# Local and global attention on one Trainium2 core: windows of 96 keys with the 32 global keys beside them as 128 rows

## The chip, the core and the metric

The kernel runs on one core of one Trainium2 chip. Its time is the device time of one execution in microseconds (us). The core has five engines that run side by side: TensorE (PE, with its weight loads PEld), VectorE (DVE), ScalarE (ACT), GpSimd (POOL) and SyncE (SP), which here issues the transfers between the memory of the chip and the on-chip memory. Matmuls write into the accumulator memory PSUM, of 8 banks; DVE and ACT read it from there.

## What is computed

Eight batches of eight heads, 512 local and 32 global tokens, 64 columns a head. A local query sees the 32 global keys and the local keys up to 32 positions away; a global query sees all 544 keys. What comes out is the input of a feed-forward layer with a gate, which is most of the work and isn't touched by the change.

```python
def _attn_ref(q_l, k_l, v_l, q_g, k_g, v_g):
    window = 32
    scale = 1.0 / np.sqrt(D)
    k_all = np.concatenate([k_g, k_l], axis=2)
    v_all = np.concatenate([v_g, v_l], axis=2)
    s_g = scale * np.matmul(q_g, k_all.transpose(0, 1, 3, 2))
    out_g = np.matmul(sm(s_g), v_all)
    s_ll = scale * np.matmul(q_l, k_l.transpose(0, 1, 3, 2))
    mask = np.abs(pos[:, None] - pos[None, :]) <= window
    s_ll = np.where(mask, s_ll, -1000000000.0)
    s_lg = scale * np.matmul(q_l, k_g.transpose(0, 1, 3, 2))
    a_l = sm(np.concatenate([s_lg, s_ll], axis=-1))
    out_l = np.matmul(a_l, np.concatenate([v_g, v_l], axis=2))
    return np.concatenate([out_g, out_l], axis=2)

def _moe_ref(x, mu_k, mu_r, w_k, w_v, w_r):
    xk = mu_k * x + (1.0 - mu_k) * x_prev
    xr = mu_r * x + (1.0 - mu_r) * x_prev
    k = np.maximum(xk @ w_k, 0.0)
    v = k * k @ w_v
    return 1.0 / (1.0 + np.exp(-(xr @ w_r))) * v
```

## The kernel before

**Units and pairs.** A unit is two heads of one batch: 32 units, 4 a batch. Two units are handled together as a pair (`attention`, L761), 16 pairs in all. The first batch is done by halves of the queries at the start (L851 on), while the weights are still coming in. From the second batch on, the attention of one batch runs beside the feed-forward part of the batch ahead: `together` (L804) hands out the steps of the two in turn, and a scheduler then orders each engine's instructions. `Run` (L354) ties the matmuls of one stage into a run that stands on TensorE without others in between; from the third batch on its first matmul waits for the readers that it is given.

**Scores** (`scores`, L308). A unit's 512 queries are 8 blocks of 64 (`BL`), each against a window of 128 local keys and the 32 global ones, 160 columns (`WG`). A matmul has 64 rows (one head's columns) by 64 queries as its weights and streams the 160 keys; two heads and two blocks use the four quarters of the array. A unit has 16 such matmuls, in four PSUM banks. DVE adds the mask, takes the row's lowest value and evacuates (L333); ACT takes the exponentials and their sum (L339); POOL multiplies by the inverse sum (L349), for the window into `Pt` and, apart from it, for the 32 global columns into `Pgl`.

**Transposes.** For each unit TensorE transposes 8 tiles of `Pt` (L394) and 2 of `Pgl` (L403), and copies bring them into `PT` and `PTg`. `scores_global` (L411) makes the scores of the global queries of both units, in 576 columns; `transposes_global` (L438) transposes them as 5 tiles into `PG`.

**Weighted sums** (`weighted`, L450). With a window's values as weights (128 keys by 64 columns of one head) a matmul streams 64 columns of `PT`; 32 of them a pair. 20 more, with the same kind of weights, stream 32 columns of `PG` for the global queries, and 8, with the global values as weights, stream 128 columns of `PTg` for the global keys' part. ACT and DVE copy the results into `xT` and `xg_all`, the feed-forward layer's input.

**Transfers.** SP issues, in order, `raw_qk` and `raw_v` for each unit, pieces `a` of the value weights from `scratch`, and the output. Only `kernel` on the host lays out keys and values: windows overlap, so values are stored more than once.

**Names in the profile.** L508 to L510 and L670 are the feed-forward matmuls. L361, L365 and L367 are the three calls in `Run.matmul`, so that all matmuls of scores and weighted sums stand under these lines: `ps<-raw_qk` are scores, `PT,raw_v`, `PG,raw_v` and `PTg,raw_v` the three kinds of weighted sums.

Of the kernel before, what the change touches and what calls it, by code (L numbers as in the profile page):

```python
# [9 lines left out]
F32 = mybir.dt.float32  # L10
# [9 lines left out]
P = 128  # L20
D = 64
SG = 32
SL = 512
BL = 64
NB = SL // BL
W = 128
WG = W + SG

SPANS = ((0, W), (32, 224), (160, 352), (288, 480), (SL - W, SL))
START = tuple(224 * (i // 2) + (128 if i % 2 else 0) for i in range(NB))
SK = START[-1] + WG

FIRST = tuple(min(max(BL * i - SG, 0), SL - W) for i in range(NB))

PAIRS = tuple(tuple((e + 4 * p, e + 4 * p + 2) for p in range(2)) for e in range(2))
# [3 lines left out]


VG0 = 2 * NB * D
VX0 = VG0 + 2 * D
NV = VX0 + 2 * D
# [10 lines left out]
def local_global_attention_then_rwkv_ffn(  # L56
# [61 lines left out]
    masks = const.tile([P, 2, 2, WG], BF16, name="masks")  # L118
    nc.gpsimd.memset(masks, 0.0)
    for e in range(2):  # L120
        for p in range(2):
            for a, i in enumerate(PAIRS[e][p]):

                m = masks[a * BL:(a + 1) * BL, e, p, SG * e:SG * e + W]
                ahead = FIRST[i] - BL * i + SG
                nc.gpsimd.affine_select(
                    out=m, in_=m, pattern=[[1, W]], base=ahead, channel_multiplier=-1,
                    compare_op=ALU.is_ge, fill=NEG,
                )
                nc.gpsimd.affine_select(  # L130
                    out=m, in_=m, pattern=[[-1, W]], base=2 * SG - ahead, channel_multiplier=1,
                    compare_op=ALU.is_ge, fill=NEG,
                )

    low = const.tile([P, 3 * W], BF16, name="low")
    nc.gpsimd.memset(low[:, 0:SG], NEG)
    nc.gpsimd.memset(low[:, SG:], 0.0)
# [15 lines left out]
    for side, n in (("left", 16), ("right", 104)):  # L153
        shift = ctx.enter_context(tc.tile_pool(name=f"shift_{side}", bufs=1, side=side))
        shift.tile([P, n], F32, name=f"shift_{side}")
# [129 lines left out]
    def load_v(s, pool=rawp, tag=""):  # L285
        raw = pool.tile([P, NV], F32, tag="v" + tag, name="raw_v")
        nc.sync.dma_start(out=raw, in_=v[s.b, s.c])
        s.v = raw[:, 0:VG0].rearrange("p (h i d) -> p h i d", h=2, d=D)
        s.vg = raw[:, VG0:VX0]
        s.vx = raw[:, VX0:NV].rearrange("p (h d) -> p h d", h=2)  # L290
# [9 lines left out]
    EACH = [(e, t, h, 4 * e + 2 * t + h) for t in range(2) for e in range(2) for h in range(2)]  # L300

    class Scores:
        def __init__(self, slots):
            self.slots = slots
            for t, (s, p) in enumerate(slots):
                s.at[p] = self, t
# [753 lines left out]
```

## Time and profile before

| | us |
|---|---|
| median of 3 runs | 691.82 |
| the runs | 690.74, 691.82, 691.88 |
| span of the profiled execution, first to last instruction | 689.8 |
| TensorE clock granted in it, mean share | 0.992 |

No time of its own is kept for the profiled execution; its span is 2.0 us below the median of the runs. The page's second part shows that TensorE and its weight loads are dense from the second slice of 17 us to the last, and that the transfers come in bursts:

```profile
PE   6979999999998999999999999999999999999997
PEld 3769789989897999999999989999999999999997
DVE  5795977457557566545675657645575656377531
DMA  8734353154737740544818092735727090535666
```

Each digit is the busy share of a fortieth of the span in tenths. In what follows, a row of a group reads: line, engine, operation, output and inputs, shape and count, then busy time in us, mean ns of one, and idle time of the engine ahead of them with what ended it.

### The profile page before, as it was taken

The numbers are of one execution on the slowest core, as the hardware profiler recorded it, in microseconds if no ns is written. First come the engines' busy times: TensorE is split into PE (matmuls) and PEld (weight loads), VectorE is DVE, ScalarE is ACT, GpSimd is POOL, SyncE is SP. The second block draws the span as 40 slices with busy tenths as digits, with TensorE's granted clock in tenths as the row PEclk, the third lists the DMA queues.
The fourth block names the chain that finished last, engine by engine and source line by source line (L and its number), as shares of the span: only waits on it lengthen the run. The fifth ranks groups of instructions, "written<-read, shape, count | busy, mean of one in ns | idle before, by whom it ended". The sixth has DMA issues, their size and how long they took to land.

```text
span 689.8 us, 18729 instructions
## 1 busy us (share of the span) xinstructions
PE 663.3 (96%) x7530; PEld 626.6 (91%) x7530; DVE 425.9 (62%) x1221; ACT 387.5 (56%) x1058; POOL 359.4 (52%) x363
## 2 busy tenths in 40 slices
PE   6979999999998999999999999999999999999997
PEld 3769789989897999999999989999999999999997
DVE  5795977457557566545675657645575656377531
ACT  5876866366355565757457563747466644443530
POOL 5577595147777344565338244655348332642810
PEclk9989999999999999999999999999999999999999
DMA  8734353154737740544818092735727090535666
GB/s 343 299 122 169 124 196 127 48 185 141 254 131 253 248 157 29 210 159 151 310 67 302 12 358 92 263 105 204 256 97 271 2 334 34 200 119 172 207 197 208
DMA packets 43542, 123.37 MB, mean 179 GB/s; under 512 B 4032, under 2 KB 20928, under 8 KB 43456
## 3 DMA queue, kind: packets, MB, share of 16 engines
q1 hardware_dynamic: 43456, 122.18, 50.0%
q8 instruction: 59, 0.97, 0.5%
q14 instruction: 27, 0.22, 0.1%
HBM read 104.86 MB, written 17.30 MB: 177 GB/s over the span
## 4 chain that ended last, share of the span: by engine, by line
PE 67%; DVE 12%; POOL 7%; DMA 6%; issue 3%; ACT 3%; SPq 0%; POOLq 0%; ACTq 0%; DVEq 0%
PE ps_m L670 16%; PE ps_m L508 11%; PE ps_m L509 11%; PE ps_m L510 11%; PE ps_s L365 9%; DMA a<-scratch 4%; PE ps_t L394 3%; DVE xfull L539 2%; DVE Pt L333 2%; PE ps_t L361 2%; DVE diff L535 2%; PE ps_s L367 2%; DMA w<-w_k 1%; DVE B L651 1%; POOL Pt L349 1%
## 5 line engine op out<-in xcount | busy, mean ns | idle before, releaser
L508 PE MATMUL ps_m<-xkh,wk_h 128*128 128x256 f32 x544 | 154.3, 285 | 3.3 <-DVE xfull L539 3.3
L509 PE MATMUL ps_m<-xkl,wk_h 128*128 128x256 f32 x544 | 153.2, 282 | 1.0 <-POOL xkl L544 1.0
L510 PE MATMUL ps_m<-xkh,wk_l 128*128 128x256 f32 x544 | 152.5, 281 | 0.0
L670 PE MATMUL ps_m<-bh,a 128*128 128x256 f32 x736 | 137.5, 282 | 3.2 <-DMA a<-scratch 3.1
L339 ACT ACTIVATE Pt<-Pt,m 128x160 f32<-128x160 f32 x256 | 106.5, 419 | 26.7 <-DVE m L333 26.7
L670 PEld LDWEIGHTS ps_m<-bh,a 128*128 128x128 f32 x736 | 114.9, 188 | 6.1 <-DMA a<-scratch 3.7
L349 POOL TENSOR_TENSOR Pt<-Pt,ssum 128x512 f32<-128x512 f32 x64 | 67.4, 1053 | 80.7 <-DVE ssum L295 32.4
L508 PEld LDWEIGHTS ps_m<-xkh,wk_h 128*128 128x128 f32 x544 | 103.0, 190 | 4.9 <-ACT xkh L543 3.8
L509 PEld LDWEIGHTS ps_m<-xkl,wk_h 128*128 128x128 f32 x544 | 102.8, 189 | 2.5 <-POOL xkl L544 1.7
L510 PEld LDWEIGHTS ps_m<-xkh,wk_l 128*128 128x128 f32 x544 | 102.8, 189 | 0.0
L670 PE MATMUL ps_m<-bl,a 128*128 128x256 f32 x368 | 102.5, 279 | 0.0
L544 POOL TENSOR_TENSOR xkl<-xfull,xkh 128x512 fp32r<-128x512 f32 x34 | 46.8, 1375 | 85.9 <-ACT xkh L543 80.9
L582 DVE TENSOR_TENSOR B<-ps_m,relu 128x512 f32<-128x512 f32 x52 | 35.9, 690 | 72.1 <-ACT relu L580 72.0
L580 ACT ACTIVATE relu<-ps_m 128x512 f32<-128x512 f32 x52 | 31.0, 597 | 82.9 <-PE ps_m L510 80.7
L508 PE MATMUL ps_m<-xrh,wr_h 128*128 128x256 f32 x272 | 77.3, 284 | 0.0
L509 PE MATMUL ps_m<-xrl,wr_h 128*128 128x256 f32 x272 | 76.2, 280 | 0.0
L510 PE MATMUL ps_m<-xrh,wr_l 128*128 128x256 f32 x272 | 76.0, 279 | 0.0
L333 DVE CUSTOM_DVE_ANT_0 Pt<-ps_s,masks 128x160 f32<-128x160 f32 x256 | 65.9, 317 | 6.6 <-PE ps_s L365 4.9
L670 PEld LDWEIGHTS ps_m<-bl,a 128*128 128x128 f32 x368 | 69.2, 188 | 0.0
L617 POOL TENSOR_TENSOR gate<-sum,gate 128x512 f32<-128x512 f32 x18 | 26.8, 1489 | 59.7 <-DVE sum L716 39.9
L205 ACT CAST bh<-B 128x512 fp32r<-128x512 f32 x76 | 45.9, 620 | 18.0 <-PE ps_m L670 11.6
L508 PEld LDWEIGHTS ps_m<-xrh,wr_h 128*128 128x128 f32 x272 | 51.5, 189 | 1.2 <-ACT kkh L564 0.6
(146 smaller groups left out, 1594.6 us busy)
## 6 DMA issues: line engine op xcount, KB each, us to landing
a<-scratch SPq DMA_DIRECT2D x92, 512.0 KB, 5.9
raw_qk<-qk SPq DMA_DIRECT2D x32, 768.0 KB, 5.6
raw_v<-v SPq DMA_DIRECT2D x32, 640.0 KB, 6.0
out_l<-gate SPq DMA_DIRECT2D x32, 256.0 KB, 4.6
w<-w_k SPq DMA_DIRECT2D x8, 512.0 KB, 9.7
w<-w_v SPq DMA_DIRECT2D x8, 512.0 KB, 3.9
w<-w_r SPq DMA_DIRECT2D x4, 512.0 KB, 3.5
scratch<-wv_h SPq DMA_DIRECT2D x8, 256.0 KB, 2.8
```

The costliest lines, as they stand in the source:

```text
L205: nc.scalar.copy(hi, val)
L333: read = nc.vector.tensor_tensor_reduce(out=Pt[:, i], in0=place(e, t, h), in1=masks[:, e, slots[t][1]], op0=ALU.add, op1=ALU.min, scale=-s ...
L339: nc.scalar.activation(Pt[:, i], Pt[:, i], AF.Exp, bias=low_x[:, i:i + 1], scale=-1.0, accum_out=ssum[:, i:i + 1],)
L349: nc.gpsimd.tensor_mul(out, Pt[:, each, at:at + n], rinv.unsqueeze(2).to_broadcast([P, 4, n]))
L365: self.last = nc.tensor.matmul(*a, **kw)
L508: nc.tensor.matmul(out, w_h[:, i, cols], x_h(i), start=(i == 0), stop=False)
L509: nc.tensor.matmul(out, w_h[:, i, cols], x_l(i), start=False, stop=False)
L510: nc.tensor.matmul(out, w_l[:, i, cols], x_h(i), start=False, stop=(i == n - 1))
L544: nc.gpsimd.tensor_sub(lo[:, both], xf, hi[:, both].bitcast(F32))
L580: nc.scalar.activation(rk, kp, AF.Relu)
L582: nc.vector.tensor_mul(k2[f0 // HC][f0 % HC // 2], kp, rk)
L670: nc.tensor.matmul(out[:, j], w, x[:, i % 2], start=fresh and (i, j, n) == (0, 0, 0), stop=(i, n) == (HC - 1, 2), skip_group_check=True,)
```

## The change

The 512 local tokens become 16 chunks of 32 (`CK`). On the host, keys and values are laid out in one order, three local chunks, then the 32 global ones, then the next three (`ORDER`), so that any four consecutive chunks are three local chunks and the global one: 14 windows of 128 rows (`START`), one for each local chunk but the two at the ends, which share their neighbour's. A query chunk's window holds all that it sees.

```diff
-BL = 64
-W = 128
-WG = W + SG
+CK = 32
+NCK = SL // CK
+W = 4 * CK
+ORDER = [x for c in range(0, NCK, 3) for x in (*range(c, min(c + 3, NCK)), None)][:-1]
+SK = CK * len(ORDER)
+NW = NCK - 2
+START = tuple(CK * (w + w // 3) for w in range(NW))
+def window_of(i):
+    return min(max(i - 1, 0), NW - 1)
+ROWS = ((2, 3, 0, 1), (4, 5, 6, 7), (8, 9, 10, 11), (14, 15, 12, 13))
-NV = VX0 + 2 * D
+NV = 2 * NW * D
```

`raw_qk` goes from 1536 to 1248 columns and `raw_v` from 1280 to 1792, of 4 bytes on 128 rows each.

A scores matmul now has 32 queries as weights and streams 128 keys; four query chunks (`ROWS`) stand in the four column groups of the array, and a unit needs two PSUM banks where it needed four. Masks are built chunk by chunk.

```diff
-        banks = [psum("s") for _ in range(4)]
+        banks = [psum("s") for _ in range(2)]
...
-                            place(e, t, h)[a * BL:(a + 1) * BL], s.q[rows, i * BL:(i + 1) * BL],
-                            s.k[rows, START[i]:START[i] + WG], start=True, stop=True,
+                            place(t, n, h)[r_ * CK:(r_ + 1) * CK], s.q[rows, i * CK:(i + 1) * CK],
+                            s.k[rows, at:at + W], start=True, stop=True,
...
-            window = Pt[:, each, SG * e:SG * e + W]
-            for out, at in ((window, SG * e), (Pgl[:, e], 0 if e else W)):
-                n = out.shape[2]
-                nc.gpsimd.tensor_mul(out, Pt[:, each, at:at + n], rinv.unsqueeze(2).to_broadcast([P, 4, n]))
+            nc.gpsimd.tensor_mul(
+                Pt[:, each], Pt[:, each], all_inv[:, each].unsqueeze(2).to_broadcast([P, 4, W])
+            )
```

`Pgl`, `PTg` and `transposes_of_g` are gone. `PT` is one fixed tile for both units, with room between its blocks for the transposed scores of the global queries (`TAIL`), which are copied in there: six transposes, of 96 keys or 128, each key once (544 columns where 576 were). In `weighted` a window's values are loaded once and stream the columns of the chunks that use the window, and behind them, in six of the 14 windows, the 32 of the global queries (`GROUPS`; `cells` makes an access of two blocks that lie apart).

```diff
-        windows(0)
-        og = global_ones() if PG is not None else None
-        windows(1)
-        for j, s in enumerate(units):
-            for e in range(2):
-                for p in pairs:
...
-                        op[t][:, j, e], s.vg[rows], r.PTg[rows, e], start=False,
+            for w, here, t in GROUPS:
...
+                    if len(here) == 1 and t is not None:
+                        i, = here
+                        moving = cells(P_of, PLACE[i], TAIL[t] - PLACE[i], 2)
+                        out = cells(out, of.index(i) * CK, (of.index(None) - of.index(i)) * CK, 2)
...
+                    run.matmul(out, s.v[:, h, w], moving, start=first, stop=True, skip_group_check=True)
```

In `attention` the scores of both units of the next pair are one run, and the scores of its global queries stand in one run with the weighted sums of this pair:

```diff
-            if nxt:
-                R.append(scores(whole(nxt[0])))
...
             if nxt:
-                R.append(scores(whole(nxt[1])))
-                Pg = scores_global(nxt)
+                run = run_of(nxt[0])
+                R = [scores(whole(s), run) for s in nxt]
             yield
+            yield
+            run = run_of(pair[0], A.copies + C.copies + copies)
             with tc.issue_after(last.ins):
-                weighted(pair, xTs, PG,
-                         copies=A.copies + C.copies + [copy] if pair[0].b > 1 else None)
+                if nxt:
+                    Pg = scores_global(nxt, run=run)
+                weighted(pair, xTs, PG, run=run)
```

What this makes of the order of instructions is shown at three places. First TensorE at the weighted sums of a pair in the middle of the program: before, the scores of the global queries (64 by 160, 32 and 384), the three kinds of weighted sums, and a unit's first transposes.

```order
L367 MATMUL ps_s<-raw_qk 64x160
L365 MATMUL ps_s<-raw_qk 64x160
L365 MATMUL ps_s<-raw_qk 64x32 x2
L365 MATMUL ps_s<-raw_qk 64x384 x2
L367 MATMUL ps_s<-PT,raw_v 64x64
L365 MATMUL ps_s<-PT,raw_v 64x64 x15
L365 MATMUL ps_s<-PG,raw_v 64x32 x20
L365 MATMUL ps_s<-PT,raw_v 64x64 x16
L365 MATMUL ps_s<-PTg,raw_v 128x2x64 x8
L394 MATMUL ps_t<-ident,Pt 128x128 x4
```

At the same place now (L371 and L373 are the lines of `Run.matmul` after the change, L703 is a feed-forward matmul):

```order
L373 MATMUL ps_s<-raw_qk 64x480
L371 MATMUL ps_s<-raw_qk 64x480
L371 MATMUL ps_t<-raw_qk 64x64 x2
L371 MATMUL ps_s<-PT,raw_v 64x96 x2
L371 MATMUL ps_s<-PT,raw_v 64x2x32 x8
L371 MATMUL ps_s<-PT,raw_v 64x96 x2
L371 MATMUL ps_s<-PT,raw_v 64x32 x32
L371 MATMUL ps_s<-PT,raw_v 64x96 x2
L371 MATMUL ps_s<-PT,raw_v 64x2x32 x8
L371 MATMUL ps_s<-PT,raw_v 64x96 x2
L703 MATMUL ps_m<-bh,a 128x256
```

60 weighted matmuls of the pair have become 56; the products with `PG` and `PTg` have gone into those with `PT`, and feed-forward matmuls stand ahead of the next transposes.

Second, TensorE at the scores. Before, one unit's 16 matmuls stand between its pair's transposes and feed-forward matmuls, and the other unit's stand some 130 rows further on:

```order
L394 MATMUL ps_t<-ident,Pt 128x128 x4
L367 MATMUL ps_s<-raw_qk 64x160
L365 MATMUL ps_s<-raw_qk 64x160 x15
L670 MATMUL ps_m<-bh,a 128x256
L670 MATMUL ps_m<-bl,a 128x256
```

Now both units' 64 stand together, followed by the last three transposes of the global queries' scores:

```order
L543 MATMUL ps_m<-xkh,wk_l 128x256
L373 MATMUL ps_s<-raw_qk 32x128
L371 MATMUL ps_s<-raw_qk 32x128 x63
L462 MATMUL ps_t<-ident,Pg 96x128 x3
L541 MATMUL ps_m<-xkh,wk_h 128x256
```

After these stand 48 or 72 feed-forward matmuls, then the run of the weighted sums shown above.

Third, ScalarE at about the same place (`relu`, `gate`, `xkh` and `xrh` belong to the feed-forward part). Before:

```order
L580 ACTIVATE relu<-ps_m 128x512
L543 CAST xkh<-xfull 128x512
L446 COPY PG<-ps_t 128x512
L339 ACTIVATE Pt,ssum<-Pt,m 128x160 x4
L595 ACTIVATE gate<-ps_m 128x512
L339 ACTIVATE Pt,ssum<-Pt,m 128x160 x2
L446 COPY PG<-ps_t 128x128
```

Now:

```order
L613 ACTIVATE relu<-ps_m 128x512
L219 CAST bh<-T_5413 128x512
L347 ACTIVATE Pt,ssum<-Pt,m 128x128 x10
L464 COPY PT<-ps_t 96x4x96
L347 ACTIVATE Pt,ssum<-Pt,m 128x128 x6
L613 ACTIVATE relu<-ps_m 128x512
L576 CAST xkh<-xfull 128x512
```

The sixteen exponentials of both units have come together, with the copy of the last global transposes (L464), for which the weighted run waits, behind ten of them.

More of the change, by code (lines that the diff above doesn't have):

```diff
@@ L450, in weighted, with cells, tails @@
[L450 to L452 removed]
+    def cells(x, at, step, n, size=CK):
+        one = x[:, at:at + size]
+        return bass.AP(one.tensor, one.offset, (one.ap[0], (step, n), (1, size)))
+    def tails(rows, at, step, n):
+        first = PT[rows, 0, 0, at:at + CK]
+        return bass.AP(first.tensor, first.offset, (first.ap[0], (PART, 4), (step, n), (1, CK)))
```

323 lines of the change are left out of this document (164 added, 159 removed).

## The prediction

> **What bounds the kernel now.** I read the busy row of the page first, then the busy time by stage, then TensorE's own waits, and then TensorE's timeline around one pair of attention units.
>
> ```profile
> PE 663.3 (96%) x7530; PEld 626.6 (91%) x7530; DVE 425.9 (62%) x1221; ACT 387.5 (56%) x1058; POOL 359.4 (52%) x363
> 0.00:45.00 45.00, 35.99 (x440) 26.48 (x440) 31.42 (x120) 31.02 (x99) 25.32 (x47) 1.00 0.74 281
> 45.00:280.00 235.00, 225.11 (x2577) 210.70 (x2578) 156.60 (x471) 140.08 (x403) 140.88 (x141) 0.98 0.45 154
> 357.00:434.00 77.00, 75.54 (x904) 72.46 (x903) 47.73 (x146) 44.87 (x129) 38.23 (x37) 1.00 0.51 186
> PE ps_s L361 <- DMA raw_qk<-qk: 5.5, 2, 4.9
> PE ps_m L508 <- DVE xfull L539: 3.3, 1, 3.3
> PE ps_m L670 <- DMA a<-scratch: 3.1, 3, 1.5
> ```
>
> The second to fourth rows are stretches of the span, with the busy time of PE, PEld, DVE, ACT and POOL in that order, the clock, the DMA share and GB/s. One batch takes about 77 us, and in the stretch from 357 to 434 us TensorE is busy for 75.5 of 77.0 at full clock, while the other engines are below 48. Its longest waits on any one cause are 5.5, 3.3 and 3.1 us, two of them in the start. So outside the first 45 us the time is TensorE's stream, and what the change takes out of that stream comes off the span, as long as nothing else grows a wait.
>
> TensorE's stream for one pair of units (two units are handled together, 16 pairs in all) looks like this; each matmul of the attention stands as two records.
>
> ```profile
> 356.81 0.35 PE L367 MATMUL ps_s<-raw_qk 128*64 128x160 f32 x1
> 357.89 0.22 PE L367 MATMUL ps_s<-PT,raw_v 128*64 128x64 f32 x1
> 357.90 0.22 PE L365 MATMUL ps_s<-PT,raw_v 128*64 128x64 f32 x1
> 357.95 0.22 PE L367 MATMUL ps_s<-PT,raw_v 128*64 128x64 f32 x1
> 358.82 1.31 PE L365 MATMUL ps_s<-PG,raw_v 128*64 128x32 f32 x40
> 359.96 1.13 PE L365 MATMUL ps_s<-PT,raw_v 128*64 128x64 f32 x32
> 361.02 1.16 PE L365 MATMUL ps_s<-PTg,raw_v 64*128 64x128 f32 x16
> 362.12 0.66 PE L394 MATMUL ps_t<-ident,Pt 128*128 128x128 f32 x4
> 362.53 0.37 PE L670 MATMUL ps_m<-bh,a 128*128 128x256 f32 x1
> 403.91 0.28 PE L670 MATMUL ps_m<-bh,a 128*128 128x256 f32 x1
> 404.12 0.35 PE L367 MATMUL ps_s<-raw_qk 64*64 64x160 f32 x1
> 368.26 0.35 PE L367 MATMUL ps_s<-raw_qk 64*64 64x160 f32 x1
> 368.26 0.36 PE L365 MATMUL ps_s<-raw_qk 64*64 64x160 f32 x3
> 368.45 1.12 PE L365 MATMUL ps_s<-raw_qk 64*64 64x160 f32 x27
> 369.50 0.38 PE L670 MATMUL ps_m<-bh,a 128*128 128x256 f32 x1
> ```
>
> Columns: start and length in us, then line, tiles, shape, count. At 357.89 and 357.90 two records start together, one on each half of the array's columns, and the next two come 0.057 us later: the array works in **rounds**. With 32 columns streamed (PG), 40 records are 20 rounds, whose last starts 0.22 before the end: (1.31 - 0.22) / 19 = 0.057 us a round. With 64 columns (PT) 32 records are 16 rounds: (1.13 - 0.22) / 15 = 0.061. So half the columns cost the same, and 32 columns pay for 64. In the scores (64 rows by 64 columns of the array) four records start at 368.26; 28 later ones are 7 rounds of four, (1.12 - 0.30) / 6 = 0.137 us a round for 160 columns.
>
> **The change part by part.** Numbers are for one pair.
>
> *Scores.* Before: 32 records a unit, 8 rounds, 369.50 - 368.26 = 1.24 us, twice: 2.48. Now a unit has 32 matmuls of 32 queries by 128 keys, 64 records, 128 for a pair, and they use quarters of the array's columns: eight tiles where there were four. If all eight run side by side, that is 16 rounds, each 128/160 of 0.137 = 0.109. The first round keeps its 0.19 (368.26 to 368.45) and the exit its 0.09 (1.24 less 0.19 less 7 x 0.137): 0.19 + 15 x 0.109 + 0.09 = 1.92. That is 0.56 less. Both units now go in one run, so one entry goes (403.91 to 404.12 is 0.21 where feed-forward matmuls follow each other in 0.11): 0.10 less. No row shows eight tiles; the bounds are 0.109 a round and, if each record costs what a PG record costs (0.057 / 2 = 0.0287), 128 x 0.0287 = 3.67 us. I take the first, since within one round of four, records start 0.02 us or less apart, so nothing spaces them by 0.0287.
>
> *Weighted sums.* Before, from 357.89 to 362.12: 4.23 us, of which the global keys' own product PTg takes 361.02 to 362.12. That product goes, and so do the 20 PG matmuls: their 32 columns ride behind the window's on the same weights. Now 56 matmuls, 112 records, 56 rounds of two. Of these 48 stream 32 or 64 columns, at 0.057: 2.74. Eight stream 96 columns, which no row shows: between 0.057 and 96/160 of 0.137 = 0.082; I take the upper, as a stream longer than 64 columns is likelier to be what binds: 0.66. With the exit of 0.15 that stood between the last PT (359.96 + 1.13 - 0.22 = 360.87) and 361.02, the sum is 3.55: 0.68 less, or 0.88 at the other bound.
>
> *Scores of the global queries.* 356.81 to 357.89, 1.08 us for 576 columns; now 544: 0.06 less.
>
> *Transposes.* 25 a pair become 22.
>
> ```profile
> 350.14 0.66 PE L445 MATMUL ps_t<-ident,Pg 128*128 128x128 f32 x4
> 350.55 0.37 PE L508 MATMUL ps_m<-xrh,wr_h 128*128 128x256 f32 x1
> 353.71 0.27 PE L445 MATMUL ps_t<-ident,Pg 128*128 128x128 f32 x1
> 353.74 0.37 PE L508 MATMUL ps_m<-xrh,wr_h 128*128 128x256 f32 x1
> 370.07 0.38 PE L403 MATMUL ps_t<-ident,Pgl 128*128 128x128 f32 x2
> 370.20 0.36 PE L670 MATMUL ps_m<-bl,a 128*128 128x256 f32 x1
> ```
>
> Four cost 0.41 until the next matmul, two 0.13, one 0.03. Before, beside the 16 of Pt: 0.13 + 0.13 + 0.41 + 0.03 = 0.70. Now two groups of three, each between 0.13 and 0.41, about 0.27: 0.54. That is 0.16 less.
>
> The pair's sum: 0.56 + 0.10 + 0.68 + 0.06 + 0.16 = **1.56 us less**. For the 14 pairs from the second batch on: 21.8 us. The first batch goes by halves; in the part after the start its second halves have 28 matmuls where 20 stood, and its scores save like the others: 0 to 1.5 less, I take 0.2.
>
> *Other engines.*
>
> ```profile
> L349 POOL TENSOR_TENSOR Pgl<-Pt,ssum 128x128 f32<-128x128 f32 x64 | 29.7, 463 | 0.0
> L404 ACT COPY PTg<-ps_t 128x256 f32<-128x256 f32 x32 | 11.6, 362 | 13.0 <-PE ps_t L403 13.0
> L333 DVE CUSTOM_DVE_ANT_0 Pt<-ps_s,masks 128x160 f32<-128x160 f32 x256 | 65.9, 317 | 6.6 <-PE ps_s L365 4.9
> L339 ACT ACTIVATE Pt<-Pt,m 128x160 f32<-128x160 f32 x256 | 106.5, 419 | 26.7 <-DVE m L333 26.7
> ```
>
> POOL loses 29.7 us and ScalarE 11.6; VectorE's masked reductions and ScalarE's exponentials get a fifth narrower. I cost all of this at nothing: it lies beside TensorE's stream. What can cost is that both units' scores come in one run, and that the weighted run stands behind the copy of the last three global transposes, which ScalarE does after ten of the sixteen exponentials. Ten take at most 10 x 0.416 (106.5 / 256) = 4.2 us, and VectorE's sixteen reductions at most 16 x 0.257 = 4.1. The cover is 48 or 72 feed-forward matmuls, 48 x 0.113 = 5.4 us or 8.1. At 48 little is left: 0 to 1 us in each of some seven pairs; I take 1.5 in all.
>
> *Transfers.*
>
> ```profile
> raw_qk<-qk SPq DMA_DIRECT2D x32, 768.0 KB, 5.6
> raw_v<-v SPq DMA_DIRECT2D x32, 640.0 KB, 6.0
> 399.66 9.09 DMA a<-scratch
> 405.00:410.00 5.00, 3.64 (x42) 3.22 (x32) 3.87 (x19) 2.92 (x13) 1.78 (x1) 1.00 1.03 402
> ```
>
> By the column counts raw_qk falls to 624 KB and raw_v rises to 896: 112 KB more a unit, 0.23 MB a pair, 0.57 us at 402 GB/s. It is paid only where TensorE already waits for a piece of scratch that shares the queues (the 3.1 us above): 0 to 6 us, I take 1.5. At the start 30-odd small selects replace 16 for the masks, in front of the first reduction: 0 to 2, I take 0.5.
>
> **Sum.** -21.8 - 0.2 + 1.5 + 1.5 + 0.5 = -18.5 on the profiled span of 689.8: 671.3. The median of the runs, 691.82, lies 2.0 above that span, which I keep: **673.3 us**. With the bounds (96 columns at 0.057: 2.8 less; no added waits: 3.5 less; the transfers' 6 and 7 of waits: 10 more) this case reaches from 667 to 683.
>
> **Rivals.**
>
> *Each record has a price of its own.* If records can't follow faster than the PG records do, the scores cost 3.67 + 0.28 = 3.95 a pair, 1.37 more than the 2.58 of before (with its extra entry); against the 0.90 of the other parts a pair loses 0.47, 14 pairs 6.6, with the 3.5 of added waits 10.1: 702 us. It decides at (2.58 + 0.90 - 0.28) / 128 = 0.025 us a record. For it: no long stretch of the trace goes below 0.0287 a record. Against it: the pattern of rounds. If it binds only part of such a run, about 695. The Trainium skill speaks for this rival: "TensorE: Matmul & The Clock Gate", section "Wait — 56ns, not 53.3ns?", has a floor of about 25 ns from start to start however few columns are streamed; by it the scores would take 3.2 us, and the whole would be an estimated 695, with no gain left. The trace doesn't hold it start by start: the first four scores records begin within 0.02 us, three of them in the row at 368.26. That 64 rows by 32 columns gives eight independent tiles is in "TensorEngine Tiling (Array Packing)", section "Available Configurations"; no run here shows it.
>
> *The gain turns into waits.* The larger run of scores holds four banks at once, and the weighted run waits for sixteen reductions and a copy behind ten exponentials. At 1 us a pair, 14 more: 687. For it: the cover of 5.4 us over 4.2 is thin. Against it: before, TensorE lost only 1.5 us in 77 to waits of this kind.
>
> **How the numbers follow.** Forecast 673, range of its own 667 to 683: 0.66. Waits, about 687: 0.17. A price per record, 690 to 702: 0.11. Below 667, since waits of before go as well: 0.06. A measurement of this kernel tells 0.2%, 1.4 us, from no change. Faster: 0.66 + 0.06 + most of the waits' case = 0.85; within: 0.05; slower: 0.10, nearly all of it the price per record. The range 664 to 688 leaves out about 0.17.
>
> **What would show it.** Scores of a pair as one block of 1.9 us with eight records a round; 3.5 us at the first rival. The weighted block at 3.5 us, with no row of PTg. A batch of 73 to 74 us instead of 77. TensorE's waits on ScalarE's copy of PT under 2 us in all, on scratch under 5. I am wrong if the round of eight is longer than 0.15 us, or if a new wait at the head of the weighted run stands in the list with 10 us.

## The result, and the profile after

The changed kernel takes 685.24 us (median of 4 runs, 683.71 to 685.79), the kernel before on the same chip 691.85 (4 runs, 690.74 to 691.89): a ratio of 0.9893, 95% interval 0.9859 to 0.9928. That is 6.6 us or 1.1% faster, in the forecast's direction and inside the stated range of 664 to 688, but above the 667 to 683 of its main case, and about a third of the 18.5 us that were forecast. Times here and below are medians of a kernel's runs, and ratios go by undisturbed runs alone: one of the four runs of e1_unmerge, the profiled one, took 1037.76 us at a granted clock of 0.56. The profiled execution has a span of 683.8 us, 6.0 below the one before, and a mean granted clock of 0.977.

The busy row of the page after:

```profile
PE 637.6 (93%) x8362; PEld 605.5 (89%) x8362; DVE 445.3 (65%) x1237; ACT 377.9 (55%) x1086; POOL 338.0 (49%) x320
```

TensorE has lost 25.7 us of busy time, more than the 22 that the sum took out of its stream, and the span lost 6.0. So the work went and the time did not: TensorE's idle time rose from 689.8 - 663.3 = 26.5 us to 683.8 - 637.6 = 46.2. ScalarE fell by 9.6 us and POOL by 21.4, as the part on other engines said in kind, but DVE rose by 19.4 us, although its masked reductions fell by 10 (65.9 to 55.9).

By stages, first of the kernel before, the four middle batches together (columns as in the prediction: length, busy time of PE, PEld, DVE, ACT and POOL, clock, DMA share, GB/s):

```profile
280.00:588.00 308.00, 304.67 (x3664) 292.57 (x3663) 185.45 (x559) 177.32 (x490) 150.76 (x145) 1.00 0.50 181
```

and of the kernel after, with the two stretches ahead of them:

```profile
0.00:45.00 45.00, 30.61 (x563) 22.98 (x564) 29.88 (x117) 29.32 (x101) 23.94 (x61) 0.92 0.75 281
45.00:280.00 235.00, 220.94 (x3093) 207.39 (x3091) 162.15 (x497) 140.60 (x432) 132.33 (x116) 0.96 0.48 168
280.00:588.00 308.00, 295.10 (x3916) 284.69 (x3915) 206.00 (x557) 173.81 (x499) 144.43 (x117) 0.99 0.53 188
```

In the middle batches TensorE stood still for 3.3 of 308 us before and for 12.9 after, and DVE's busy time there grew by 20.6 us, about as much as it grew by in all.

Some of TensorE's waits after (who waited for whom: us in total, times, longest):

```profile
PE ps_m L703 <- ACT sum L721: 6.7, 5, 2.0
PE ps_s L367 <- DMA raw_qk<-qk: 6.3, 3, 4.3
PE ps_t L406 <- ACT PT L409: 5.1, 5, 1.5
PE ps_t L462 <- ACT PT L413: 4.4, 1, 4.4
PE ps_t L406 <- DVE mg L437: 3.9, 3, 2.2
PE ps_t L367 <- DVE mg L437: 2.8, 1, 2.8
...
PE ps_m L703 <- DMA a<-scratch: 0.8, 2, 0.6
```

The wait for scratch is nearly gone here. New are the product of values behind a copy of a sum (L703, L721), and the transposes of window probabilities (L406) behind their own copies and behind L437, the second reduction of the global scores. In the middle batches these waits make up nearly all of the 12.9 us, and none of them is at the head of the weighted run, where the prediction had expected one; the single wait of 2.8 us is at the first weighted product of an early pair, at 104.6 us. The wait of 4.4 us (L462 for L413) is in the first batch, at 23.6 us. It stands in e3_old_order too, below, with 4.1, so it belongs to the new tiles and not to their order.

TensorE's timeline of one pair after, the scores and then the global scores with the weighted sums:

```profile
337.36 0.29 PE L373 MATMUL ps_s<-raw_qk 64*32 64x128 f32 x1
337.36 0.33 PE L371 MATMUL ps_s<-raw_qk 64*32 64x128 f32 x7
337.50 1.92 PE L371 MATMUL ps_s<-raw_qk 64*32 64x128 f32 x119
339.34 0.53 PE L462 MATMUL ps_t<-ident,Pg 128*96 128x128 f32 x3
339.63 0.36 PE L541 MATMUL ps_m<-xkh,wk_h 128*128 128x256 f32 x1
...
345.34 0.62 PE L373 MATMUL ps_s<-raw_qk 128*64 128x480 f32 x1
...
346.31 3.63 PE L371 MATMUL ps_s<-PT,raw_v 128*64 128x96 f32 x112
349.87 0.38 PE L541 MATMUL ps_m<-xrh,wr_h 128*128 128x256 f32 x1
```

Eight records start within the first 0.14 us, and 128 take 339.34 - 337.36 = 1.98 us: eight tiles do work side by side. The global scores take 346.31 - 345.34 = 0.97, the weighted sums 349.87 - 346.31 = 3.56.

Where the time goes instead is seen at a change of batch. Selected rows of PE, DVE, POOL and ACT from 425 to 441 us, with the idle time of the engine and what ended it in brackets:

```profile
424.79 3.35 PE L371 MATMUL ps_s<-PT,raw_v 128*64 128x64 f32 x104
427.58 1.50 DVE L684 TENSOR_TENSOR T<-B,B 128x512 f32<-128x512 f32 x1
428.50 1.74 POOL L577 TENSOR_TENSOR xkl<-xfull,xkh 128x512 fp32r<-128x512 f32 x1
429.01 1.77 DVE L684 TENSOR_TENSOR B<-B,B 128x512 f32<-128x512 f32 x1
430.70 0.87 DVE L572 SCALAR_TENSOR_TENSOR xfull<-diff,mu_r_sb,xT 128x256 f32<-128x256 f32 x2
431.50 0.27 DVE L437 CUSTOM_DVE_ANT_0 Pg<-ps_t,nothing,mg 128x64 f32<-128x64 f32 x1
431.81 0.75 ACT L441 ACTIVATE Pg<-Pg,mg 128x544 f32<-128x544 f32 x1 [4.45 <-DVE mg L437]
431.93 0.63 PE L406 MATMUL ps_t<-ident,Pt 128*128 128x128 f32 x4 [0.87 <-DVE mg L437]
432.56 0.25 ACT L528 COPY xT<-ps_s 128x128 f32<-128x128 f32 x1
435.61 0.62 ACT L576 CAST xkh<-xfull 128x512 fp32r<-128x512 f32 x1 [1.62 <-DVE xfull L572]
436.31 1.29 POOL L577 TENSOR_TENSOR xkl<-xfull,xkh 128x512 fp32r<-128x512 f32 x1 [2.38 <-ACT xkh L576]
437.64 1.91 DVE L572 SCALAR_TENSOR_TENSOR xfull<-diff,mu_r_sb,xT 128x256 f32<-128x256 f32 x2 [2.06 <-POOL xkl L577]
439.58 0.62 ACT L576 CAST xrh<-xfull 128x512 fp32r<-128x512 f32 x1 [0.39 <-DVE xfull L572]
440.62 0.58 ACT L721 COPY sum<-ps_m 128x512 f32<-128x512 f32 x1
441.25 0.55 PE L703 MATMUL ps_m<-bh,a 128*128 128x256 f32 x1 [2.05 <-ACT sum L721]
```

Read it downwards. The weighted run is over on TensorE at about 428 us, but on DVE the short reduction L437 stands behind two differences of keys (L684) and two xfull. The differences take 1.5 and 1.8 us while POOL works; the next one, at 431.87 us, with POOL idle, takes 0.68. ACT waits 4.45 us for L437, and only then copies the weighted sums out (L528). From those follow xkh, xkl, xfull and xrh, each behind the other, and behind xrh in ACT's queue stands the copy of a sum (L721) for which TensorE then waits 2.05 us. The first wait of TensorE, 0.87, is for the bank that L437 reads.

The waits have a second price. Right behind the wait that ends at 441.25 us, TensorE's granted clock is halved for 3.4 us (TensorE alone: length, busy time and records, clock, DMA share, GB/s):

```profile
441.30:444.70 3.40, 3.40 (x16) 0.50 0.16 66
```

TensorE handles 16 records there, and 32 in the 3.4 us from 444.80 on, at full clock; and the profile counts the stretch as busy. In the changed kernel, after the first 52 us, four such stretches lie at the four waits of more than 2 us (they end at 104.62, 204.68, 355.03 and 441.25 us) and add up to 17.0 us; in e3_old_order, shown below, 6.8 us are left. As an estimate, half of these lengths is lost, 8.5 and 3.4 us. It is no fixed rule: in e3_global_moved waits of 2.10 and 2.04 us, at 363 and 441 us, leave the clock at full.

Three of the groups of DVE that grew, before (differences, mixed tokens, differences of keys):

```profile
L535 DVE TENSOR_TENSOR diff<-xT 128x256 f32<-128x256 f32 x56 | 37.8, 714 | 12.2 <-ACT xT L500 12.0
L539 DVE SCALAR_TENSOR_TENSOR xfull<-diff,mu_r_sb,xT 128x256 f32<-128x256 f32 x56 | 32.6, 612 | 8.7 <-POOL xkl L544 4.8 <-POOL xrl L544 3.5
L651 DVE TENSOR_TENSOR T<-B,B 128x512 f32<-128x512 f32 x12 | 9.3, 774 | 0.2
```

and after:

```profile
L568 DVE TENSOR_TENSOR diff<-xT 128x256 f32<-128x256 f32 x56 | 42.0, 777 | 7.3 <-ACT xT L535 7.1
L572 DVE SCALAR_TENSOR_TENSOR xfull<-diff,mu_r_sb,xT 128x256 f32<-128x256 f32 x56 | 44.2, 828 | 16.3 <-POOL xkl L577 12.8 <-POOL xrl L577 3.4
L684 DVE TENSOR_TENSOR T<-B,B 128x512 f32<-128x512 f32 x12 | 11.0, 914 | 0.2
```

The same instructions in the same number take up to a third longer (612 to 828 ns). The trace shows what parts the long ones from the short: of all 136 xfull, those with POOL at work for less than a tenth of their time took 476 ns on average in both kernels (94 of them before, 66 after), those with POOL at work for over nine tenths took 969 and 915 ns (19 and 24). POOL was at work in 39% of xfull's time before, in 57% after and in 46% in e3_old_order. The masked reductions L341, which read PSUM, took 285 ns with POOL idle or at work.

### The profile page after: what moved, and what is told of

Read it like the earlier page. It is cut to its first block, busy times and chain, and to the rows that moved or that the text cites. A ratio compares the mean times of both kernels' runs of the same rounds, so it can differ in the third digit from the quotient of the medians.

```text
span 683.8 us, 20432 instructions
## 1 busy us (share of the span) xinstructions
PE 637.6 (93%) x8362; PEld 605.5 (89%) x8362; DVE 445.3 (65%) x1237; ACT 377.9 (55%) x1086; POOL 338.0 (49%) x320
## 3 DMA queue, kind: packets, MB, share of 16 engines
q8 instruction: 66, 1.08, 0.6%
## 4 chain that ended last, share of the span: by engine, by line
PE 54%; DVE 17%; ACT 13%; issue 4%; DMA 3%; POOL 3%; SPq 0%; POOLq 0%; ACTq 0%; DVEq 0%
PE ps_m L703 14%; PE ps_m L541 10%; PE ps_m L543 10%; PE ps_m L542 10%; ACT Pt L347 7%; DVE xfull L572 5%; PE ps_s L371 4%; PE ps_t L406 3%; DVE diff L568 2%; DVE B L684 2%; DVE B L615 1%; DMA w<-w_v 1%; DVE kkl L598 1%; DMA raw_qk<-qk 1%; PE ps_t L462 1%
## 5 line engine op out<-in xcount | busy, mean ns | idle before, releaser
L703 PE MATMUL ps_m<-bh,a 128*128 128x256 f32 x736 | 139.3, 285 | 7.5 <-ACT sum L721 6.7
L703 PEld LDWEIGHTS ps_m<-bh,a 128*128 128x128 f32 x736 | 117.2, 193 | 9.8 <-ACT sum L721 7.7
L347 ACT ACTIVATE Pt<-Pt,m 128x128 f32<-128x128 f32 x256 | 99.3, 390 | 16.9 <-DVE m L341 16.8
L703 PE MATMUL ps_m<-bl,a 128*128 128x256 f32 x368 | 103.8, 282 | 0.0
L703 PEld LDWEIGHTS ps_m<-bl,a 128*128 128x128 f32 x368 | 70.7, 192 | 0.0
L341 DVE CUSTOM_DVE_ANT_0 Pt<-ps_s,masks 128x128 f32<-128x128 f32 x256 | 55.9, 285 | 4.0 <-PE ps_s L367 1.7
L572 DVE SCALAR_TENSOR_TENSOR xfull<-diff,mu_r_sb,xT 128x256 f32<-128x256 f32 x56 | 44.2, 828 | 16.3 <-POOL xkl L577 12.8
```

The costliest lines, as they stand in the source:

```text
L341: read = nc.vector.tensor_tensor_reduce(out=Pt[:, i], in0=place(t, n, h), in1=masks[:, 2 * slots[t][1] + n], op0=ALU.add, op1=ALU.min, sca ...
L347: nc.scalar.activation(Pt[:, i], Pt[:, i], AF.Exp, bias=low_x[:, i:i + 1], scale=-1.0, accum_out=ssum[:, i:i + 1],)
L572: nc.vector.scalar_tensor_tensor(self.shape(xf[:, j]), self.shape(diff[:, j]), mu[:, c0 + j:c0 + j + 1], self.prev(c0 + j), op0=ALU.mult, ...
L703: nc.tensor.matmul(out[:, j], w, x[:, i % 2], start=fresh and (i, j, n) == (0, 0, 0), stop=(i, n) == (HC - 1, 2), skip_group_check=True,)
```

## The experiments

Three theories stood at the start. **1**: both units' scores in one run send 16 reductions to DVE and 16 exponentials to ACT at one time, and the work at a change of tokens comes late behind them. **2**: the second piece of the global scores holds the only bank of tag t. **3**: DVE works more slowly beside POOL. Against all three: the PE work is what I mis-sized, or it is hidden and no longer counts. Times are medians; the kernel before had 691.2 to 692.2 us beside these runs, and the changed kernel itself, run again as e2_control, 687.14 us.

**Two runs of scores again.**

```diff
             for j, r in enumerate((A, C)):
                 transposes(r, 0, j)
                 yield
                 transposes(r, 1, j)
                 yield
+                if nxt and j == 0:
+                    R.append(scores(whole(nxt[0]), run_of(nxt[0])))
+                    yield
             PG, last, copies = transposes_global(Pg)
             yield
             if nxt:
-                run = run_of(nxt[0])
-                R = [scores(whole(s), run) for s in nxt]
-            yield
+                R.append(scores(whole(nxt[1]), run_of(nxt[1])))
             yield
```

> The changed kernel with one thing undone: the window scores of the next pair are made in two runs again, those of its first unit after the transposes of the first unit of this pair, those of the second where both stood. Theory 1 (the merged run sends 16 reductions to DVE and 16 exponentials to ACT in one burst, and what stands behind them, diff, xfull, B and T at a change of tokens, comes late for PE): most of the lost gain comes back, 676 to 681 us, and PE's idle time falls from 46 us to 34 or less. Theory 2 (the single bank of tag t, in which the second piece of the global scores now waits for DVE): no gain, 685 to 687 us, as the extra entry into a run costs about 0.1 us a pair. Theory 3 (contention of DVE with POOL): DVE busy stays near 445 us and the time within 2 us of 685.

681.13 us, ratio to before 0.982 (0.9776 to 0.9865): at the upper edge of what theory 1 expects. The trace of the same edit is e2_unmerge, below.

**The second piece of the global scores in another bank.**

```diff
-                    Pg = scores_global(nxt, run=run)
+                    Pg = scores_global(nxt, other="m", run=run)
```

> The changed kernel, but the 64-column piece of the global scores goes, from batch 1 on, to a bank of tag m (three banks there) and not to the only bank of tag t. Theory 2 (the bank): the waits of the transposes for L437, 3.9 + 2.8 us in the changed kernel, are gone, and the time is 679 to 682.5 us. Theory 1 (the burst): the reduction L437 is late whatever bank it reads, so that a wait of the same size stands before a feed-forward bank instead; 684 to 687 us.

689.78 us, ratio 0.9984 (0.996 to 1.0007), above both expectations. The waits on L437 are gone, and the wait of L703 for the copies of sums is 9.2 us instead of 6.7. New waits stand in the global scores themselves, two of 4.2 and 2.8 us, for a bank that a feed-forward tile holds. So this run exchanges one bank's waits for another's, and does not settle theory 2 alone. e2_unmerge and e3_old_order, below, do: they keep the bank, and their waits on L437 are 0.5 us and none.

**More work for TensorE.**

```diff
                 last = nc.tensor.transpose(tp[:hi - lo, n], Pg[:, lo:hi], ident)
+            for _ in range(4):
+                with tc.issue_after(last.ins):
+                    last = nc.tensor.transpose(bank[:, 3 * P:], ident, ident)
```

> The changed kernel with PE work added and nothing else: four more transposes of the identity into the unused quarter of the bank behind each of the two groups of transposes of the global probabilities, eight a pair, by 0.11 us some 0.9 us a pair and 12 us over 14 pairs. If PE no longer sets the pace in the middle batches (theories 1 to 3 all say that waits do), the time grows by 0 to 5 us, to 685 to 690. If PE is still the bound there and the sizes of the matrix work are what I have wrong, it grows by 10 to 13 us, to 695 to 698.

707.85 us, 20.7 above the control: outside both ranges. A wait in its trace tells why it can't answer:

```profile
ACT PT L468 <- PE ps_t L466: 15.9, 13, 6.2
```

L466 are the added records, and ACT's copy out of the bank waited for them. So this lengthened the way from transposes to weighted sums as well. The last pair of experiments asks the question again.

**POOL's division left out** (batches 1 to 7, so the window probabilities aren't divided by their sums).

```diff
-        for h in range(2):
+        for h in range(0 if slots[0][0].b else 2):
             each = slice(4 * h, 4 * h + 4)
             nc.gpsimd.tensor_mul(
```

> The changed kernel without POOL's division of the window probabilities by their sums in batches 1 to 7 (this part of the computation is left out): 56 POOL instructions of 1.09 us less, 61 us of POOL. Theory 3 (DVE's diff and xfull, 420 to 475 ns alone, take 1.2 to 1.5 us when a POOL multiply runs beside them, and this holds the batch boundary up): DVE busy falls from 445 to 432 us or less and the time to 678 to 682. Theories 1 and 2: the transposes get their operand 1 to 2 us earlier, but the burst and the bank stay; 682 to 685 us, DVE busy above 438 us.

681.29 us, ratio 0.9856 (0.9788 to 0.9925), and DVE 425.7 us busy: what theory 3 expects. In the middle batches:

```profile
280.00:588.00 308.00, 298.46 (x3950) 288.37 (x3949) 188.44 (x556) 175.19 (x499) 116.87 (x92) 0.99 0.54 191
```

DVE is back at 188 us from 206, with the same instructions. So its extra time is time beside POOL. It doesn't show that this is all: the edit also takes some 1.1 us out of the way from exponentials to transposes. And DVE's extra time is not what makes the largest wait: TensorE still waits 6.8 us for the copies of sums (L703 for L721), with DVE as short as before.

**The control.**

> The changed kernel itself, so that small differences are read against it on the same chip. Every theory expects 684 to 687 us, and in the middle batches two stalls of PE in each, of 1 to 2.4 us: a group of transposes of window probabilities behind the weighted run, and a product of values behind a copy of a sum.

687.14 us (683.49 to 688.96), ratio 0.9928 (0.9907 to 0.995), just above the expected 684 to 687, with both kinds of stall at the same places.

**Two runs of scores, with a profile.** The edit is that of e1_unmerge.

> The window scores of the next pair in two runs again, as in e1_unmerge, whose profile was disturbed. Theory 1 (the burst of 16 reductions and 16 exponentials holds DVE's boundary work up, and this PE): 677 to 682 us, PE idle at least 8 us below the control's, the stalls behind the weighted run under 1 us each. Theory 3 (DVE beside POOL) without the burst: the stalls stay, within 2 us of the control, and diff and xfull have the same mean durations as in the control. If both work through the same queue, the time falls, and DVE's busy time with it.

682.14 us (four runs, 676.33 to 684.93), ratio 0.9848 (0.978 to 0.9916): 5.0 below the control, at the upper edge of theory 1's range, as e1_unmerge was. Of its middle batches, and of TensorE's waits:

```profile
280.00:588.00 308.00, 299.42 (x3962) 288.08 (x3961) 187.07 (x554) 173.96 (x495) 150.21 (x120) 1.00 0.52 193
```

```profile
PE ps_m L703 <- DMA a<-scratch: 7.0, 8, 1.8
...
PE ps_s L373 <- DVE m L341: 3.1, 5, 0.9
```

With all of POOL's work in place DVE is at 187 us: the place of the scores alone brings its work beside POOL's or takes it away. As far as DVE's time goes, theories 1 and 3 are one: the burst is what puts DVE's boundary work beside POOL's. TensorE is idle for 8.6 us of the stretch, between the 3.3 of before and the 12.9 of after; what is left are waits for scratch and, at the head of the run with the global scores, for reductions.

The 7.0 us for scratch, 0.7 in e3_old_order below, come with the place of the global scores. They are the last to read `raw_qk`, and SP's next load of `raw_qk` waits for them. At one such wait, of 1.75 us at 398.00, the load goes out at 384.80, 1.7 us ahead of `raw_v`, with the pieces of scratch behind both. In e3_old_order the same load goes out 5.0 us ahead of `raw_v` (378.21 and 383.23), and TensorE waits 0.16 us for scratch. That the later load makes the wait was not tested by a run of its own.

**The second piece beside the weighted sums**, in columns that their first bank leaves free, so that no bank is taken for it (allocated ahead as `hold`).

```diff
-        sp = [psum(bank)[:, :FIRST_K], psum(other)[:, :NGK - FIRST_K]]
+        sp = [psum(bank)[:, :FIRST_K], (psum(other) if hold is None else hold[0])[:, FIRST_K - NGK:]]
...
-        both = [psum("o") for _ in range(2 if 2 * n_s > SL else 1)]
+        both = hold or [psum("o") for _ in range(2 if 2 * n_s > SL else 1)]
```

> The 64-column piece of the global scores goes to columns that the first bank of the weighted sums leaves free, so that no bank is taken for it at all and no transposes can wait for its reduction. If that wait (3.9 + 2.8 us in the changed kernel) is a loss by itself: 679 to 682 us. If it only stands where the lateness of DVE shows first, the lateness shows at the next place (the copies behind diff and xfull, the product of values behind a copy of a sum): 683 to 687 us, with the waits for copies of sums at 7 us or more.

699.44 us, ratio 1.0124 (1.006 to 1.0188): slower than before, and both expectations missed. TensorE's largest wait:

```profile
PE ps_s L371 <- DVE mg L437: 12.4, 6, 3.5
```

The weighted sums now wait for the reduction that reads their bank, and with DVE behind, each such wait takes up to 3.5 us in the run itself.

**Both edits.**

> Both edits together, two runs and the 64-column piece beside the weighted sums. If the two act apart, their gains add: 673 to 678 us. If both only make room before the same boundary work of DVE, no more than the better of the two: 677 to 682 us.

679.23 us, ratio 0.9812 (0.9782 to 0.9842). That is what the second case expects. The same bank costs nothing here: of the waits on L437 two are left, of 0.6 and 0.5 us at 78 and 165 us, none of them in the middle batches. So a wait on L437 is not a matter of its bank but of how late DVE is.

**Two runs at one place.**

```diff
-                run = run_of(nxt[0])
-                R = [scores(whole(s), run) for s in nxt]
+                R = [scores(whole(nxt[0]), run_of(nxt[0]))]
+                R += [scores(whole(nxt[1]), run_of(nxt[1]))]
```

> The changed kernel with the window scores of the two units as two runs, but both still at the place of the merged one, right after one another in the program. If it is the place (16 reductions and 16 exponentials asked for at one time) that costs: as the control, 685 to 688 us, DVE busy 441 us or more. If it is the single run on PE (128 records that nothing can come between): as e2_unmerge, 679 to 683 us.

687.49 us, ratio 0.994 (0.9908 to 0.9972), the time that the first case expects, with DVE busy for 438.4 us, under its 441. The wait for the copies of sums (L721) is 1.0 us here, and another stands in its place:

```profile
PE ps_s L373 <- DVE m L341: 12.3, 8, 2.0
```

A run's first matmul waits for the last reduction that was asked for before it (`run_of`). The trace has this wait at the first global scores, at the head of the run with the weighted sums (2.03 us at 353.03, for one): the second unit's eight reductions now stand on DVE behind differences and xfull, from 351.12 on. It is 12.3 / 8 = 1.5 us each of eight times. So the lateness of DVE only meets TensorE at another place, the one that the prediction named, and the time does not tell the place from the single run.

**The whole order of the kernel before.** The edit of e1_unmerge, and the global scores again with the scores of the second unit:

```diff
             if nxt:
-                R.append(scores(whole(nxt[1]), run_of(nxt[1])))
+                run = run_of(nxt[1])
+                R.append(scores(whole(nxt[1]), run))
+                Pg = scores_global(nxt, run=run)
...
             with tc.issue_after(last.ins):
-                if nxt:
-                    Pg = scores_global(nxt, run=run)
                 weighted(pair, xTs, PG, run=run)
```

> The whole order of the kernel before with the new tiles: window scores at two places, and the global scores of the next pair with the second of them instead of ahead of the weighted sums. If the change's order is the whole loss, this is what I forecast for the tiles alone: 672 to 677 us. If the place of the global scores does nothing: 680 to 684 us, as e2_unmerge.

**674.63 us** (674.21 to 675.72), ratio 0.9751 (0.9716 to 0.9786): 17.6 below the kernel before and 12.5 below the control, the fastest of all. Its busy row, middle batches and one of its waits (that for scratch is 0.7 us):

```profile
PE 642.7 (96%) x8362; PEld 605.1 (90%) x8362; DVE 427.5 (64%) x1237; ACT 378.5 (56%) x1086; POOL 340.5 (51%) x320
```

```profile
280.00:588.00 308.00, 305.91 (x4009) 293.40 (x4009) 187.84 (x558) 174.86 (x497) 150.15 (x121) 1.00 0.55 189
```

```profile
PE ps_s L373 <- DVE m L341: 2.2, 4, 0.6
```

TensorE is idle for 2.1 of the 308 us, and it gets through 4009 records there where the changed kernel got through 3916. No wait on L437, on L721 or on the copies L409 is left in its list. TensorE's mean granted clock is 0.989, against 0.977 in the changed kernel.

**The place of the global scores alone**, window scores merged:

```diff
-                R = [scores(whole(s), run) for s in nxt]
+                R = [scores(whole(s), run) for s in nxt]
+                Pg = scores_global(nxt, run=run)
...
-                if nxt:
-                    Pg = scores_global(nxt, run=run)
```

> The other half alone: the window scores stay merged, and the global scores go back from the run of the weighted sums to the run of the scores. If DVE's lateness at the reduction L437 is what PE waits for, it is read earlier here and its waits go: 679 to 683 us. If the burst is the cause, the two reductions only join it: 685 to 690 us.

692.51 us, ratio 1.0011 (0.9983 to 1.0038): all of the gain is gone, 2.5 us above what the second case expects. Its two largest waits:

```profile
PE ps_s L371 <- DVE m L341: 7.5, 9, 2.1
PE ps_m L703 <- ACT sum L721: 7.3, 5, 2.1
```

The window scores hold all four banks of tag s; a global piece behind them in the same run needs one of them, and waits until DVE has read it. The wait for L721 is about as long as in the control (7.7), although L437 is done here before the copies of the weighted sums are due (at 426.2 us, ahead of the stall at 441.47).

**POOL's division left out, with two runs.**

> e2_unmerge without POOL's division of the window probabilities by their sums in batches 1 to 7 (left out, as in e1_no_norm, where it was worth some 6 us on the merged kernel). If contention of POOL with DVE is a loss beside the burst, it is worth as much here: 674 to 678 us, DVE busy 420 us or less. If it only prices the burst (DVE's work lies beside POOL's because 16 exponentials end together): 680 to 683 us, DVE busy 425 us or more.

676.47 us, ratio 0.979 (0.9739 to 0.9841), as the first case expects. By the medians it is 5.7 below e2_unmerge, as much as on the merged kernel (687.14 to 681.29, 5.9), though the intervals of the two ratios overlap; DVE's busy time in all fell from 430.0 to 417.7. So POOL's division is worth something beside the burst too, and how far by contention with DVE, how far as a step on the way to the transposes, stays open.

**More work for TensorE, again**, this time two transposes of each group done twice ahead of the others, in the changed kernel and in e3_old_order.

```diff
-        for i in range(4):
+        for i in ((0, 1) if j is not None else ()) + (0, 1, 2, 3):
             last = nc.tensor.transpose(tp[:, i * P:(i + 1) * P], r.Pt[:, 4 * h + i], ident)
```

> The changed kernel with two of the four transposes of each group of window probabilities done twice, ahead of the four (eight more a pair by 0.109 us, 12 us over 14 pairs). If PE's work still counts in full there and the new stalls stand beside it: 696 to 701 us. If the stalls come from work of DVE and ACT that goes on meanwhile, so that PE's work hides in them: 686 to 693 us.

> The same added work in e3_old_order, the new tiles in the order of the kernel before. If PE sets its pace, as it did in the kernel before, the 12 us count in full: 684 to 689 us. If even there a part of PE's time is waiting that can take work in: 675 to 682 us.

696.94 us, 9.8 above the control, and 683.42, 8.8 above e3_old_order. The first is what the case of counting in full expects, the second lies a little below its range. By these medians about four fifths and three quarters of the 12 us count. So TensorE's work was not hidden in the changed kernel: what the tiles save is saved, and the stalls of the new order are added to it.

The order's two parts side by side, with the new tiles in all four:

| window scores | global scores ahead of the weighted sums (the change) | global scores with the second window scores (as before) |
|---|---|---|
| one run for both units (the change) | 687.1 | 692.5 |
| two runs at two places (as before) | 682.1 | 674.6 |

Each part of the old order helps or hurts by what the other is; together they are worth 12.5 us. DVE's busy time goes with the row: 445.9 and 442.6 us in the first, 430.0 and 427.5 in the second. So does the wait for L721, 7.7 and 7.3 us against none: both come with the merged window scores. The place of the global scores acts through other waits: on L437 in the control (6.6 us), for banks of tag s in e3_global_moved (7.5), for scratch in e2_unmerge (7.0).

## Why the prediction was wrong

*What bounds the kernel* held: TensorE's stream was the time, and added work still counts by most of its length.

*Scores*: forecast 1.92 us, measured 1.98. *Weighted sums*: 3.55, measured 3.56. *Global scores*: 0.06 less was forecast, 1.08 to 0.97 is 0.11. *Transposes*: 0.27 for a group of three, measured 339.63 - 339.34 = 0.29. The sum of -21.8 for the pairs was about right in size: tiles alone, in the old order, gave 17.6 us in the time, with TensorE's busy time 20.6 lower and its idle time, in a span of 672.9, 30.2 instead of 26.5.

*Transfers*: +1.5 was forecast, and the wait for scratch fell from 3.1 to 0.8 us in the changed kernel and to 0.7 in e3_old_order. In e2_unmerge it is 7.0, with transfers of the same sizes, so what it costs hangs on the order and not on the larger raw_v alone. *Masks*, +0.5: no run parts them from the rest; in the first 45 us DVE's busy time fell (31.42 to 29.88) and POOL's too (25.32 to 23.94). The clock there is 0.92 instead of 1.00, but so it is in e3_old_order, so there it is not what parts the two orders; after the first 52 us it parts them by an estimated 5 us at most (8.5 less 3.4, above).

*The step that failed* is the one on the other engines: "I cost all of this at nothing: it lies beside TensorE's stream", with 1.5 us for the waits of the new order. The order costs 12.5 (687.14 - 674.63). I had asked whether sixteen reductions and ten exponentials fit under the feed-forward matmuls ahead of the weighted run, and in the changed kernel's middle batches they do: its head has no such wait. I had not asked what stands behind them on DVE and ACT. There it is the differences of keys, diff and xfull of the next tokens, and, by the move of the global scores into the weighted run, the reduction L437, with the copies of the weighted sums behind that. These fell into one another's queue and beside POOL's work, and DVE's busy time rose by 20.6 us in the middle batches. In the rows shown TensorE met the lateness 4 and 13 us after the weighted run, at L406 and L703.

The links of that chain are not of equal weight. The wait at L703 stays at 6.8 us when DVE's extra time is taken away (e1_no_norm) and at 7.3 when L437 is moved (e3_global_moved), and is gone in e2_unmerge and e3_old_order, where the two units' scores are apart. (In e2_g_in_sums, where TensorE already waits in the weighted run, it is 1.1.) So it comes with the merged scores. What e1_no_norm and e3_global_moved have in common is ACT's copy of the weighted sums (L528). DVE makes small copies of them too (L519, L520), which stand behind the differences and xfull, and L528 waits that long for DVE: 4.16 us in e1_no_norm (at 426.12) and 4.59 in e3_global_moved (at 432.55). In e3_old_order DVE is through with the differences at 419.43 us, while the weighted run is still on, and the same copy waits 0.44 us (at 422.24).

DVE at 62% busy over the span had read as room; the room was not at the change of batch.

*The rivals.* A price per record fell: 1.98 us for 128 records is 0.0155 us a record, well under the 0.025 at which it decided. The Trainium skill's floor of about 25 ns from start to start ("TensorE: Matmul & The Clock Gate", section "Wait — 56ns, not 53.3ns?") would make 3.2 us of it; here the measurement decides against it for records that go to eight tiles. Waits in place of the gain was the case that came, at 685 against its 687, with the wrong place named: in the middle batches it is not the weighted run that waits. Its number was 1 us at each of 14 heads of that run, so that it came out near is luck.

*What would show it*: a batch of 73 to 74 us was named. The changed kernel does not show it (its stalls at L703, at 364.27, 441.25 and 516.93 us, lie 77.0 and 75.7 apart). e3_old_order does; its weighted runs at the same phase begin at these times (rows of its timeline):

```profile
345.37 0.30 PE L373 MATMUL ps_s<-PT,raw_v 128*64 128x96 f32 x1 [0.52 <-DVE m L341]
...
418.88 0.30 PE L373 MATMUL ps_s<-PT,raw_v 128*64 128x96 f32 x1 [0.52 <-DVE m L341]
```

That is 73.5 us; the next is at 491.99, 73.1 us later. TensorE's waits on the copies of PT, said to stay under 2 us, are 5.1 in the changed kernel. Neither sign of being wrong came: 16 rounds in 1.98 us are shorter than 0.15 us each, and no wait of 10 us stands at the head of the changed kernel's weighted run.

## What to carry to other kernels

When a change to tiles also moves steps, price the two apart, and for a moved step ask of every engine that it feeds what stands behind it in that engine's queue, up to the next place where the bound engine waits for that queue. Ask also how long the step now holds the buffers that it reads. A share of busy time over the span says nothing of the room at a boundary where several steps come due at once. Where a change gains less than its work, try its new tiles in the old order first: here that is one experiment, it shows nearly all of the missing gain (17.6 of 18.5 us), and it is the faster kernel.

## What was not expected of the hardware

DVE's instructions from SBUF (the on-chip memory beside PSUM) to SBUF have no fixed price: the differences T took 686 ns on average in e3_old_order and 914 in the changed kernel, with 1500 in the row above, where POOL worked beside it; the order alone moved that mean by a third. The masked reductions, which read PSUM, kept their 285 ns. A wait of TensorE of some 2 us can be followed by 3.4 us at half clock, which idle time does not show. Eight tiles of 64 rows by 32 columns start eight records at once, 16 rounds in 1.98 us. And 12 us of work added to TensorE cost 8.8 us in e3_old_order, where it was 96% busy, and 9.8 in the changed kernel, where it was 93% busy.
